# An mLSTM cell with a SwiGLU feed-forward: a new start-up order, M and decay spread from bf16 parts, wider weight pieces, the third group's k and q by 32x32 tiles, the last result by columns

## The chip, the cores and the metric

The kernel runs on one core of a Trainium2 chip (trn2). Time is the device time of one execution in microseconds (us). Before the change it is 604.95 us (median of 3 runs, 604.86 to 605.26).

Engines: PE = TensorE, PEld = its weight loads, DVE = VectorE, ACT = ScalarE, POOL = GpSimd, SP = SyncE, which here only issues transfers. L12 is line 12 of that kernel; the same statement has another line number in another kernel.

## The reference

```python
# q, k, v, o_gate: (4, 8, 768, 40) float32; i_gate, f_gate: (4, 8, 768) float32
for t in range(S):                                   # the mLSTM cell
    m_new  = np.maximum(f_gate[:, :, t] + m, i_gate[:, :, t])
    f_stab = np.exp(f_gate[:, :, t] + m - m_new)
    i_stab = np.exp(i_gate[:, :, t] - m_new)
    C = f_stab * C + i_stab * np.einsum('bhd,bhe->bhde', vt, kt)
    n = f_stab * n + i_stab * kt
    h_tilde = np.einsum('bhde,bhe->bhd', C, qt)
    denom = np.maximum(np.abs((n * qt).sum()), 1.0)
    y[:, :, t] = sigmoid(o_gate[:, :, t]) * h_tilde / denom
x = y.transpose(0, 2, 1, 3).reshape(3072, 320)       # the bridge
g = x @ w_gate                                       # (320, 1536)
out = (g * sigmoid(g) * (x @ w_val)) @ w_out         # (1536, 320)
# [cut: axes of broadcasting.] The three weights arrive as float64.
```

## The kernel before

The cell is computed in chunks of 128 steps. A unit is one batch entry and one chunk, 24 in all, and three units make a group. The program is a start-up, in which the first two groups of the cell, the conversion of all weights from float64 and the first group of the feed-forward are done, and then seven more groups.

Each piece of work is a Python generator, and a string says which generator makes its next step. Each engine executes its instructions in that order, so the string is the schedule. Names in it: `R` loads a weight piece, `C` converts it, `kq` loads k and q, `T` turns (transposes) them, `M` and `E` spread M (the running maximum, `m` in the reference) and the decay, that is, copy one head's row to all partitions, `S` scores, `F` finish of a unit, `H` gate and value products, `J` the products with w_out.

```python
START = """
pad0 kq1*2 pad0 bar1 v1 pad1 bar2 kq1 pad2 pad4 kq1 pad4 pad5 pad2 which kq0*2 runA v2 ... [cut]
"""

def convert(n):                       # float64 bits to float32: ACT twice, DVE three times, POOL once
    ...
    nc.scalar.activation(bits, hi.bitcast(F32), AF.Abs)
    nc.scalar.activation(low, lo, AF.Identity, scale=2.0 ** -51, bias=two_c)
    yield
    nc.vector.tensor_scalar(bits, bits, scalar1=2.0 ** -15, scalar2=None, op0=ALU.max)
    nc.vector.tensor_scalar(bits, bits, scalar1=3, scalar2=None, op0=ALU.logical_shift_left)
    nc.vector.scalar_tensor_tensor(size, in0=hi, scalar=0x80000000, in1=bits, ...)
    yield
    nc.gpsimd.tensor_tensor(place(*key).bitcast(U32), low, size, op=ALU.add)   # wgv_sb or wo_sb
    yield

def spread_m(u):                      # one head's row of M to all 128 partitions, float32
    ...
            nc.tensor.matmul(units[u]["mb"][two][:, j, :], lhsT=idb[:, h:h + 1].to_broadcast([BH, 128]),
                             rhs=M_sb[:, c, :], start=False, stop=True, skip_group_check=True)

def turn(u, tag):                     # k and q: four PE transposes each, one ACT copy each
    ...
            for j in range(PR):
                nc.tensor.transpose(tp[:, j, :], un[name][:, 2 * j:2 * j + 2, :]..., ident)
            yield
            nc.scalar.copy(un[name + "T"], tp)
            yield

def project(g, i, part):              # h times w_out, a third of the contraction at a time
    ...
    for m in range(part * n, (part + 1) * n):
        nc.tensor.matmul(p, lhsT=h_ring[...], rhs=wo["sb"][:, m, :], start=(m == 0), stop=(m == NFC - 1))
    yield
    if part == 2:
        nc.scalar.copy(z, p)
        yield
        nc.sync.dma_start(out=out[ds(g * TW + i * 128, 128), :].rearrange("(t four) d -> four t d", four=NSQ), in_=z)
        yield
```

The groups from the fourth on already take k and q another way: loads that lay 32x32 tiles side by side, which DVE then transposes (`load_x`, `turn_x`). A float32 matmul instruction shows as two PE records in these traces.

## Time and profile before

| | before |
|---|---|
| median of the first 3 runs | 604.95 us |
| span of the profiled run | 603.9 us |
| PE busy | 580.7 us (96%) |
| first feed-forward products of units 1 and 2 (t0) | 62.4 us |
| first products of the second group (g2) | 139.1 us |
| second group | 66.9 us, PE without a gap |
| DVE, ACT, POOL busy | 52%, 38%, 28% |

At **t0** the matmuls of the form 64x256 begin, the feed-forward of units 1 and 2. At **g2** the second group begins; from there to the end PE works back to back. Shares of busy time over the whole span say little here: DVE at 52% looks idle, yet it decides t0.

### The profile page before, as it was taken

Reading aid. Unit: us, or ns where it says so; the run is one execution under the profiler, and the core shown is the slowest. Engines: PE = TensorE matmul, PEld = TensorE weight load, DVE = VectorE, ACT = ScalarE, POOL = GpSimd, SP = SyncE. Lnnn points to the kernel's source line nnn. Section 1 sums busy time; section 2 is a strip of 40 time slices with the busy share of each in tenths; the row PEclk is TensorE's granted clock in tenths of the full one; section 3 lists DMA queues with packets and bytes.
Section 4 is the critical chain, followed back from the end, with each engine's and each line's share of the span. In section 5 each row is a group of like instructions: output and inputs, shape, how many; then the busy total and the mean of one; then the engine's idle time right before and its main releaser. Section 6 shows DMA issues by size and latency. Waiting matters only on the chain.

```text
span 603.9 us, 11003 instructions
## 1 busy us (share of the span) xinstructions
PE 580.7 (96%) x4132; PEld 393.9 (65%) x4132; DVE 316.0 (52%) x742; ACT 227.8 (38%) x484; POOL 167.2 (28%) x236
## 2 busy tenths in 40 slices
PE   7877899999999999999999999999999999999996
PEld 5665666766657666776667666766677666766564
DVE  7289778972457345552467245644466334633310
ACT  3736799974215321433224411542143411111100
POOL 4235565570213221251213222151114211220000
PEclk9878799999999999999999999999999999999999
DMA  9798999504631166104651267005740300010000
GB/s 134 199 127 187 213 206 219 150 13 93 109 89 41 55 113 120 64 12 90 91 111 47 64 109 138 36 11 106 106 116 13 90 18 0 3 30 4 1 6 26
DMA packets 150612, 50.74 MB, mean 84 GB/s; under 512 B 126592, under 2 KB 145376, under 8 KB 150432
## 3 DMA queue, kind: packets, MB, share of 16 engines
q1 hardware_dynamic: 150560, 50.05, 40.8%
q8 instruction: 32, 0.52, 0.4%
q14 instruction: 20, 0.16, 0.1%
HBM read 45.91 MB, written 4.11 MB: 83 GB/s over the span
## 4 chain that ended last, share of the span: by engine, by line
PE 85%; DVE 5%; DMA 3%; ACT 2%; POOL 2%; issue 1%; SPq 1%; DVEq 0%; ACTq 0%; POOLq 0%
PE gv_ps L605 48%; PE o_ps L624 23%; PE yT L517 5%; PE sp L498 3%; PE add L543 2%; PE mb L443 2%; PE tp_kq L486 1%; DMA raw<-in_moe_w_out_dram 1%; POOL wo_sb L297 1%; DMA e_bc<-e_dram 1%; DMA v<-in_v_dram 1%; ACT w_sb L472 1%; DMA out_dram<-z_sb 1%; DVE size L293 0%; DVE bits L292 0%
## 5 line engine op out<-in xcount | busy, mean ns | idle before, releaser
L605 PE MATMUL gv_ps<-xT,wgv_sb 64*128 64x384 f32 (+2 forms) x1980 | 323.5, 480 | 9.7 <-DVE xT L591 3.5
L605 PEld LDWEIGHTS gv_ps<-xT,wgv_sb 64*128 64x128 f32 x1980 | 193.2, 192 | 126.2 <-POOL wgv_sb L297 6.4
L624 PE MATMUL o_ps<-wo_sb,h_ring 128*128 128x320 f32 x576 | 158.0, 434 | 0.9 <-POOL wo_sb L297 0.7
L612 DVE TENSOR_TENSOR sg<-sg,gv_ps 128x384 f32<-128x384 f32 x84 | 46.5, 554 | 182.9 <-ACT sg L609 182.9
L624 PEld LDWEIGHTS o_ps<-wo_sb,h_ring 128*128 128x128 f32 x576 | 108.5, 190 | 48.1 <-POOL wo_sb L297 1.8
L609 ACT ACTIVATE sg<-gv_ps 128x384 f32<-128x384 f32 (+2 forms) x99 | 47.6, 481 | 233.5 <-PE gv_ps L605 233.4
L577 POOL TENSOR_TENSOR yb<-yb,o 128x512 f32<-128x512 f32 x24 | 30.4, 1267 | 120.5 <-DVE yl L576 120.5
L613 DVE TENSOR_TENSOR h_ring<-sg,gv_ps 128x384 f32<-128x384 f32 (+2 forms) x99 | 53.5, 541 | 12.7 <-ACT sg L609 3.2
L506 POOL TENSOR_TENSOR qT<-qT,e_bc 128x512 f32<-128x512 f32 x18 | 22.9, 1274 | 118.1 <-PE sp L498 58.2
L472 ACT ACTIVATE w_sb<-w_sb,g_T 128x128 f32<-128x128 f32 x168 | 51.1, 388 | 6.3 <-POOL w_sb L468 6.2
L584 ACT COPY yb<-yb 32x512 f32<-32x512 f32 x24 | 14.8, 616 | 60.3 <-POOL yb L577 60.0
L502 DVE TENSOR_TENSOR w_sb<-sp,w_sb 128x512 f32<-128x512 f32 x48 | 31.0, 684 | 7.5 <-POOL v_w L477 4.5
L468 POOL TENSOR_SCALAR_AFFINE_SELECT w_sb<-w_sb 128x1024 f32<-128x1024 f32 x21 | 22.9, 1091 | 41.6 <-DMA w_sb<-M_dram 40.9
L591 DVE STREAM_TRANSPOSE xT<-yb 128x512 f32<-128x512 f32 x24 | 17.1, 710 | 31.0 <-POOL yb L584 30.2
L498 PEld LDWEIGHTS sp<-qT,kT 64*128 64x128 f32 x384 | 27.1, 199 | 6.1 <-issue 0.7
L498 PE MATMUL sp<-qT,kT 64*128 64x128 f32 x384 | 28.7, 287 | 0.1
L629 ACT COPY z_sb<-o_ps 128x320 f32<-128x320 f32 x24 | 10.1, 421 | 48.2 <-issue 25.3
L202 POOL COPY lo<-o 32x128 f32<-32x128 f32 x48 | 19.0, 395 | 33.4 <-ACT o L199 29.5
L517 PE MATMUL yT<-w_sb,v 128*64 128x128 f32 x384 | 27.5, 282 | 0.0
L297 POOL TENSOR_TENSOR wgv_sb<-low,size 128x512 uint32<-128x512 uint32 (+1 forms) x16 | 19.2, 1201 | 21.6 <-DVE size L293 20.6
L517 PEld LDWEIGHTS yT<-w_sb,v 128*64 128x64 f32 x384 | 23.8, 141 | 1.1 <-issue 1.1
L564 DVE STREAM_TRANSPOSE yb<-yT 128x256 f32<-128x256 f32 x48 | 18.8, 427 | 7.4 <-PE yT L517 7.4
(87 smaller groups left out, 436.2 us busy)
## 6 DMA issues: line engine op xcount, KB each, us to landing
w_sb<-M_dram SPq DMA_DIRECT2D x21, 512.0 KB
e_bc<-e_dram SPq DMA_DIRECT2D x36, 128.0 KB
k<-in_k_dram SPq DMA_DIRECT2D x48, 80.0 KB
v<-in_v_dram SPq DMA_DIRECT2D x24, 160.0 KB
o<-in_o_gate_dram SPq DMA_DIRECT2D x48, 80.0 KB
raw<-in_moe_w_out_dram SPq DMA_DIRECT2D x8, 480.0 KB
out_dram<-z_sb SPq DMA_DIRECT2D x24, 160.0 KB
raw<-in_moe_w_gate_dram SPq DMA_DIRECT2D x24, 128.0 KB
```

The costliest lines, as they stand in the source:

```text
L297: nc.gpsimd.tensor_tensor(place(*key).bitcast(U32), low, size, op=ALU.add)
L468: nc.gpsimd.affine_select(w, w, compare_op=ALU.is_ge, fill=-NEG, base=0, pattern=[[0, H], [1, L]], channel_multiplier=-1)
L472: nc.scalar.activation(w[:, h], m[h], AF.Exp, bias=g_T[:, c, b * H + h:b * H + h + 1], scale=-1.0)
L498: nc.tensor.matmul(sps[two][:, j, :], lhsT=un["kT"][r, j, :], rhs=un["qT"][r, j, :], start=True, stop=True)
L502: nc.vector.tensor_tensor(w2, un["sp"][two], w2, op=ALU.mult)
L517: nc.tensor.matmul(un["ys"][two][col * HP:(col + 1) * HP, (h % PR) // 2, :], lhsT=lhsT, rhs=rhs, start=(two, col) in un["fresh"], stop=las ...
L577: (nc.gpsimd if u in GATED else nc.vector).tensor_tensor(yb, yb, un["o"].rearrange("p x (four d) -> p x four d", d=D)[:, :, :, 0:32], op=A ...
L605: nc.tensor.matmul(ps[i][:, cols], lhsT=wgv_sb[r, kc, ts(m, 128)], rhs=xts[g][r, kc, cols], start=(kc == 0), stop=(kc == NKC - 1))
L609: nc.scalar.activation(sg[:, cols], ps[0][:, cols], AF.Sigmoid if g else AF.Silu)
L612: nc.vector.tensor_tensor(sg[:, cols], sg[:, cols], ps[0][:, cols], op=ALU.mult)
L613: nc.vector.tensor_tensor(h_ring[:, (g * NFC + m) % NH, cols], sg[:, cols], ps[1][:, cols], op=ALU.mult)
L624: nc.tensor.matmul(p, lhsT=h_ring[:, (g * NFC + m) % NH, ts(i, 128)], rhs=wo["sb"][:, m, :], start=(m == 0), stop=(m == NFC - 1))
```

## The change

The start-up loses PE passes (float32 spreading, 24 transposes), gets wider weight loads, and an order in which four conversions come early and ACT changes its table less often. The last result is written in two column halves.

Core of the diff (cuts marked `...`):

```diff
-    f_sb = gates.tile([BH, NB, L], F32)
-    nc.sync.dma_start(out=f_sb, in_=f_gate.rearrange("b h (c t) -> (b h) c t", t=L))
+    f_sb = gates.tile([128, NB, L], F32)          # copies in partition quarters 0, 2, 3
+    for c0, c1, quarters in ((0, GC, (0, 2, 3)), (GC, NB, (0,))):
+        for r in quarters:
+            for t, a in ((f_sb, f_gate), (i_sb, i_gate)):
+                (nc.scalar if r else nc.sync).dma_start(out=t[r * BH:(r + 1) * BH, c0:c1], in_=...)
...
+    def upper(t):                                 # the upper 16 bits of each float32, as bf16
+        return t.bitcast(BF16).rearrange("p c (t two) -> p c t two", two=2)[:, :, :, 1]
+
+    def parts(t, n):                              # quarter 2: the rest, quarter 3: the rest of that
+        for r in (64, 96):
+            x = t[r:128, 0:n]
+            nc.vector.tensor_tensor(x, x, upper(x), op=ALU.subtract)
+        yield
...
     def spread_m(u):                              # spread_e likewise
-                nc.tensor.matmul(units[u]["mb"][two][:, j, :], lhsT=idb[:, h:h + 1].to_broadcast([BH, 128]),
-                                 rhs=M_sb[:, c, :], start=False, stop=True, skip_group_check=True)
+                nc.tensor.matmul(units[u]["mb"][two][:, j, :], lhsT=ones(h, 128),
+                                 rhs=upper(M_sb)[:, c, :], start=False, stop=True, skip_group_check=True)
...
+        if m < 2:
+            piece("gv", 0, PR, m * 128, 128)
+        elif m % 2 == 0:
+            for a in range(0, PR, 2):
+                piece("gv", a, 2, m * 128, 256)   # was: PR blocks of rows, 128 columns
...
-            nc.scalar.copy(un[name + "T"], tp)
+            if u in first and name == "k":
+                nc.vector.tensor_copy(un["kT"], tp)
+            else:
+                nc.scalar.copy(un[name + "T"], tp)
...
+            if c > 0 and u in early:              # the C update of the first two groups
+                nc.gpsimd.tensor_tensor(kept, old[:, :, 0:D1], d, op=ALU.mult)
+                yield
+                nc.vector.tensor_tensor(new[:, :, 0:D1], add, kept, op=ALU.add)
...
-            nc.vector.tensor_copy(den[p:p + 32], den[p + 32:p + HP])
+            (nc.gpsimd if u in early else nc.vector).tensor_copy(den[p:p + 32], den[p + 32:p + HP])
...
+    def project_last(g, i):
+        n = DM // 2
+        for c, copy in enumerate((nc.scalar.copy, nc.vector.tensor_copy)):
+            for m in range(NFC):
+                nc.tensor.matmul(p, lhsT=h_ring[...], rhs=wo["sb"][:, m, ts(c, n)], ...)
+            yield
+            copy(z, p)
+            yield
+            dst = out[ds(g * TW + i * 128, 128), ts(c, n)].rearrange("(t four) d -> four t d", four=NSQ)
+            for r in range(NSQ):
+                (nc.sync if r % 2 else nc.scalar).dma_start(out=dst[r], in_=z[r * 32:(r + 1) * 32])
+            yield
...
-    for u in first + second + third:              # T: PE transposes
+    for u in first + second:
         stream(f"kq{u}", load_kq, u)
         stream(f"T{u}", turn, u, "cell")
+    stream("X", place_x)
+    for n in range(4):
+        stream(f"x{n}", load_x, 2, n)
+    for u in third:
+        stream(f"k{u}", load_k, u)
...
+        if g == 1:
+            for n, u in enumerate(third):
+                stream(f"t{n}", turn_x, u)
+        play(GROUP1 if g == 1 else GROUP, streams)
```

The string START is new as a whole, and GROUP1 is GROUP with the third group's turning and k loads placed in the second group.

## The prediction

> **What bounds the kernel now.** I read the page's busy table and the 40 slices first, then a table of stretches, the chain, the matmul groups by shape, and last the order of PE and DVE instructions in time over the first 140 us.
>
> ```profile
> PE   7877899999999999999999999999999999999996
> ACT  3736799974215321433224411542143411111100
> PEclk9878799999999999999999999999999999999999
> DMA  9798999504631166104651267005740300010000
> ```
>
> PE is full from the fifth slice to the last but one. Only the first four slices (60 us) have gaps, and there the clock dips too.
>
> The stretches (columns: window, length, then busy us of PE, PEld, DVE, ACT, POOL with counts, granted clock, DMA share, GB/s):
>
> ```profile
> 0.00:20.00 20.00, 16.03 (x70) 12.30 (x71) 12.73 (x40) 6.89 (x18) 7.77 (x34) 1.00 0.99 156
> 20.00:62.40 42.40, 30.57 (x317) 25.22 (x316) 30.07 (x73) 25.88 (x52) 18.29 (x24) 0.78 0.90 167
> 62.40:100.00 37.60, 37.50 (x270) 25.17 (x272) 29.93 (x57) 33.38 (x60) 21.67 (x24) 0.93 0.99 206
> 123.60:139.20 15.60, 15.05 (x66) 10.46 (x66) 8.80 (x17) 10.49 (x23) 9.38 (x12) 1.00 0.12 30
> 139.20:206.10 66.90, 66.90 (x490) 44.78 (x490) 33.98 (x84) 21.72 (x50) 16.08 (x22) 1.00 0.35 72
> ```
>
> The kernel has a start-up (0 to 139.2 us: the first two groups of the cell, conversion of all weights, the first group of the feed-forward, transposes for the third group) and seven further groups. The last line is one such group: PE 66.90 of 66.90 us. Six full groups, a shorter last one and the tail make 603.9 - 139.2 = 464.7 us, all PE back to back. DVE, ACT and POOL have room in it and nothing they win there is time. So the question is when the start-up ends.
>
> Inside the start-up the PE timeline shows the gaps (start, length, what, in brackets the idle before it and its releaser):
>
> ```profile
> 7.40 3.78 PE L443 MATMUL mb<-f_sb,ident 32*128 32x128 f32 x16 [0.74 <-DVE f_sb L358]
> 13.01 3.78 PE L443 MATMUL mb<-f_sb,ident 32*128 32x128 f32 x16
> ...
> 43.21 1.94 PE L605 MATMUL gv_ps<-xT,wgv_sb 64*128 64x128 f32 x20 [2.96 <-DVE C L549]
> ...
> 53.66 4.36 PE L605 MATMUL gv_ps<-xT,wgv_sb 64*128 64x128 f32 x40 [2.78 <-POOL wgv_sb L297]
> ...
> 62.38 7.22 PE L605 MATMUL gv_ps<-xT,wgv_sb 64*128 64x256 f32 x40 [3.47 <-DVE xT L591]
> ```
>
> At 62.4 the feed-forward of units 1 and 2 begins; it waits for DVE's xT, the end of `finish` of unit 2. After that PE hardly idles. I call this moment t0. DVE was busy 12.73 + 30.07 = 42.8 us before it, so idle for nearly 20, mostly between 10 and 30 us while PE spread M in float32 and ACT waited for that.
>
> **What the Trainium skill says.** (1) "FP8 and Floating Point Precision", TensorE Precision Notes: true FP32 takes 4 passes of the array. The trace agrees: an o_ps instruction of 320 columns is two records, 72 records in 19.59 us, so 0.54 us an instruction, or 4 x 320 columns at 2.35 per ns. (2) "TensorE: Matmul & The Clock Gate", What's actually happening: the array runs at 1.2 GHz until about 3.4 us of sustained work, then at 2.4. It agrees: 16 mb records take 3.78 us early, 0.236 us each, twice the 0.107 us of two passes of 128 columns at full clock. (3) "DMA: Bandwidth & Descriptors", Why small descriptors are slow: a fixed cost per packet. The trace: 6636 packets, nearly all 160 bytes, went at 128 GB/s in the first 10 us at a full share; around 20 to 30 us, with 1 KB rows, 189 GB/s at 0.80. (4) "ScalarE: Activation LUTs", Table sets: each change of set costs a load, about 2.7 us there; here each is 1.28 us. The measurement decides.
>
> **The change part by part.**
>
> M and decay: the spreading matmul becomes bf16 over 128 partitions (three exact parts, one pass). Before:
>
> ```profile
> L443 PE MATMUL mb<-f_sb,ident 32*128 32x128 f32 x48 | 10.0, 381 | 0.7 <-DVE f_sb L358 0.7
> L454 PE MATMUL e_ps<-e_sb,ident 32*64 32x128 f32 x32 | 3.1, 348 | 0.1
> L486 PE MATMUL tp_kq<-ident,k 128*128 128x128 f32 x36 | 7.1, 332 | 1.4 <-DVE f_sb L351 1.2 <-DVE w_sb L502 0.2
> ```
>
> After: 24 mb records of perhaps 0.11 to 0.16 us cold (estimate: one pass), 3 us instead of 10, and 16 of e, 1.5 instead of 3.1. It costs four DVE subtractions of about 0.5 us, two ahead of the first M spread, which moves from 7.4 to about 9.1 us; but all 24 can then be done by about 14 us where the last now ends at 22.6.
>
> Third group in 32x32 tiles: 24 PE transposes go, 24 x 0.148 us (4 in 0.59) = 3.6 us of PE at the end or middle of the saturated part, so worth their time in full. Six ACT copies of 0.59 us go too, and 1.5 us around 137 to 139 us where transposes waited for those copies. In their place 12 DVE transposes of 0.43 us in the second group, where DVE has 33 us free, and small-packet loads that have some 30 us until they are needed.
>
> Weight pieces of 256 columns: same bytes in 2 KB rows. 5.2 of the 7.9 MB of gate and value weights; 230 GB/s to perhaps 300 (estimate from the packet times above), 5 us of DMA time. Natural k, q of the third group leave the busy stretch too, 6 x 164 KB at 128 GB/s, 7.7 us.
>
> Order of the start-up: rewritten. Four conversions now come before the first score product on DVE, filling the hole of 10 to 30 us. ACT changes table 14 times instead of 18 before the second group, 5.1 us less; its work up to the last conversion falls from 101.5 to 81.4 us (counts by group times mean durations). DVE's falls from 102.7 to 96.7: den copies and half of the C update go to POOL, kT copies and the parts come.
>
> Now t0. In the new DVE order the work up to xT of unit 2 is 51.7 us by the same means; for before the same count gives 46.4 where the trace has 42.8 (neighbours overlap), so 47.7 us. Starting at 1 us with no idle that is 48.7. Following the order by hand through M, W, scores, copies and `finish`, with the durations of before, I find waits of only 1.5 to 2 us (a POOL-and-ACT tail in `finish`), 50.5. Everything slips a little, and PE will be cold: I take t0 = 53.5 against 62.4.
>
> PE work left after t0, at warm times (64x384: 0.161 us a record; x256: 0.108; o_ps 0.272; sp 0.89, yT 0.67, add 0.8 per 16):
> before: 180 x 0.161 + 60 x 0.108 + 72 x 0.272 + 36 transposes x 0.148 + sp 1.8 + yT 4.0 + add 1.6 = 67.8; 62.4 + 67.8 = 130.2, the real end was 139.2, so 9 us lost (cold clock after the gap near 3, conversions and table loads).
> after: the same without 32 of the transposes, with 1.5 us of unit 0's third piece: 64.6. With less load on ACT I take 6 us lost. 53.5 + 64.6 + 6 = 124.1. The last conversion would be at about 53.5 + 45 x 0.93 + 3 = 98, well ahead of the last products that need it.
>
> So the start-up gives 139.2 - 124.1 = 15.1 us: 8.9 from t0, 3.2 from work removed, 3 from fewer stalls.
>
> Last result by columns: two passes of 12 instructions with 160 columns. Their matmul would be 0.133 us a record, but the same weights must be loaded twice, and a 128x128 f32 transpose, load and pass, takes 0.148. So 48 x 0.148 = 7.1 against 24 x 0.272 = 6.5 us, +0.6 or up to +2.5 if the load's 0.19 us record is its rate. The tail after the last matmul (598.5 to 603.9) gains a shorter copy and half the bytes in the last transfer, perhaps 0.6. Net +0.5.
>
> Sum: 604.95 - 15.1 + 0.5 = 590.4; I say **590**.
>
> **The rivals.** (a) The early gain is taken up by a new wait: conversions placed early on in-order DVE stall everything if the weights, now sharing the first 20 us of a saturated DMA with k, q, v, come late (DMA share is already 0.99 in 0 to 20). Four pieces are 2 MB, about 9 us of DMA, and unit 1's k, q queue behind them. Then t0 stays at 59 to 62, only the removed work and the stalls count: 597 to 599. (b) PE isn't the limit after t0 but DVE is: 42 us of work in the 42 us of PE work before the o_ps; if PE waits for conversions as in before, the loss stays 9 us: 593 to 594. (c) All goes as in the hand-walk, t0 50.5 and loss 4: 585. (d) DMA binds: its share in before sums to about 110 us up to the last weight piece; minus 5, minus 7.7, minus v and w loads moved behind, it is near 90, so hidden.
>
> **Range and chances.** t0 is uncertain by 4 us, the loss by 3, the tail by 1: **583 to 598** should hold it 8 times in 10. 2% is 592.9. Faster by over 2%: 0.68; within: 0.31; slower: 0.01, since groups two to eight keep their PE work to the instruction.
>
> **What would show it.** mb x24 bf16, under 4 us and the last done before 16; the first x256 feed-forward matmuls at 50 to 57; DVE idle before them under 8 us; the second group's first matmul at 120 to 129, each later group 66.9 us; o_ps x160 records near 0.148. I am wrong if PE waits in the first 60 us for a DMA of raw weights or k, q, if the second group idles for the 32x32 loads, or if the last column parts take 2 us more than before.

## The result, and the profile after

The changed kernel took **586.38 us** (median of 4 runs, 584.98 to 586.90), beside 605.11 us for the kernel before on the same chip (4 runs). The ratio is 0.968 (95%: 0.965 to 0.971). A ratio is the mean time of one kernel's fast runs over that of the other's fast runs of the same rounds, so not quite the ratio of the medians. The prediction of 590 was 3.6 us too high, inside its range.

The page's slices after the change, 14.6 us each (busy tenths of PE and of ACT, and of the DMA engines):

```profile
PE   4797999999999999999999999999999999999997
ACT  2768789832125313341153222542153321111110
DMA  8998997455470566126710465115720300010001
```

PE is at nine tenths from the fifth slice to the last but one, as before, but a slice is shorter. ACT's dense stretch ends with the eighth slice instead of the ninth. The DMA engines are full until the sixth.

The table of stretches of the changed kernel (columns as in the prediction):

```profile
0.00:20.00 20.00, 10.16 (x60) 6.77 (x60) 17.78 (x49) 8.61 (x21) 8.14 (x32) 1.00 0.94 178
20.00:54.10 34.10, 28.21 (x274) 23.21 (x274) 28.33 (x62) 25.03 (x50) 21.46 (x38) 1.00 0.94 183
...
121.20:188.20 67.00, 67.00 (x489) 46.25 (x488) 35.05 (x88) 19.31 (x43) 15.86 (x22) 1.00 0.46 82
```

In the first 20 us DVE is busy 17.78 us where it was 12.73: the hole while PE spread M in float32 is filled. Up to t0 DVE works 17.78 + 28.33 = 46.1 of 54.1 us. The last line is the second group, as full as before.

The PE timeline of the changed kernel (start, length, what, idle before it and its releaser):

```profile
9.95 1.01 PE L504 MATMUL mb<-f_sb,ones_of 128*128 128x128 bf16 x8 [2.03 <-DMA q<-in_q_dram]
...
16.78 0.61 PE L504 MATMUL mb<-f_sb,ones_of 128*128 128x128 bf16 x4
...
54.08 5.88 PE L676 MATMUL gv_ps<-xT,wgv_sb 64*128 64x256 f32 x48 [0.94 <-DVE xT L662]
60.45 15.67 PE L676 MATMUL gv_ps<-xT,wgv_sb 64*128 64x384 f32 x92 [0.50 <-POOL wgv_sb L332]
...
121.24 8.98 PE L676 MATMUL gv_ps<-xT,wgv_sb 64*128 64x384 f32 x54
```

The last spread of M ends at 17.4 us; before it was 22.6. t0 is 54.08 us and g2 121.24.

The groups by shape of the changed kernel (busy us, mean ns of one):

```profile
L504 PE MATMUL mb<-f_sb,ones_of 128*128 128x128 bf16 x24 | 3.3, 307 | 2.0 <-DMA q<-in_q_dram 2.0
L515 PE MATMUL e_ps<-e_sb,ones_of 128*64 128x128 bf16 x16 | 1.1, 264 | 0.4 <-DVE w_sb L566 0.4
L711 PE MATMUL o_ps<-wo_sb,h_ring 128*128 128x160 f32 x48 | 6.7, 299 | 0.0
```

Spreading M and the decay costs PE 4.4 us instead of 13.1.

The spans differ by 603.9 - 584.3 = 19.6 us, and the two moments split that exactly: 62.38 - 54.08 = **8.3 us before t0**; (139.13 - 62.38) - (121.24 - 54.08) = **9.6 us between t0 and g2**; the remaining **1.7 us after g2**.

To see the middle part, here is that same stretch, t0 to g2, of each kernel. Of before:

```profile
62.38:139.13 76.75, 74.83 (x508) 51.46 (x509) 60.87 (x118) 66.86 (x124) 44.10 (x47) 0.96 0.70 156
```

And of the changed kernel:

```profile
54.08:121.24 67.16, 66.66 (x497) 47.16 (x497) 53.56 (x101) 55.93 (x110) 47.49 (x58) 1.00 0.78 184
```

The traces show PE at two speeds: four transposes of one form take 1.12 us at one place of the changed kernel (35.48) and 0.66 at another (43.48). Records at the faster speed are called warm here, at the slower one cold. The prediction counts 67.8 us of warm PE work there before and 64.6 after (an estimate from warm record lengths). Before, PE idles 76.75 - 74.83 = 1.9 us and its records are together 74.83 - 67.8 = 7.0 us longer than warm ones: 9.0 lost. After, it idles 0.5 us and the records are 2.1 us longer: 2.6 lost. ACT's busy time in the stretch fell from 66.86 to 55.93 us.

A part of the 7.0 is not the order's. In the traced run of the kernel before, PE was cold just after t0: the granted clock there was 0.52, which makes 5.62 x 0.48 = 2.7 us:

```profile
62.38:68.00 5.62, 5.62 (x28) 4.57 (x30) 4.32 (x8) 2.96 (x7) 4.20 (x5) 0.52 1.20 180
```

The first 40 records of the form 64x256 took 7.22 us there (in the prediction); in d_m below, with the same 3.5 us of idle before them and the same order after them, they took 4.59. What decides whether this cold stretch comes was not found; it did not come in the changed kernel.

Now the end. The DMA view of the last 6 us of the kernel before (598 to 604 us, 40 slices of 0.15 us; share in tenths of 16 engines, and GB/s):

```profile
DMA  0000000000000012221223222222200000000000
GB/s 0 0 0 0 0 0 0 0 0 0 0 0 0 0 34 43 17 26 17 77 94 94 77 102 102 94 102 102 102 9 0 0 0 0 0 0 0 0 0 0
```

The same view of the changed kernel, 580.5 to 584.4 us (slices of 0.1 us):

```profile
DMA  0000000000000000266103751000000000000000
GB/s 0 0 0 0 0 0 0 0 0 0 0 0 0 0 0 0 53 164 158 46 0 85 184 125 26 0 0 0 0 0 0 0 0 0 0 0 0 0 0 0
```

Before, the final transfer is 160 KB in one piece; it runs for some 2.4 us, most of it at about 100 GB/s, on two tenths of the engines. After, two short bursts of up to 184 GB/s and seven tenths. From the end of the last copy to the end of the span it took 4.9 us before and 3.0 after.

### The profile page after: what moved, and what is told of

Same layout as the page of the kernel before. It is cut to its first block, busy times and chain, and to the rows that moved or that the text cites. A ratio compares the mean times of both kernels' runs of the same rounds, so it can differ in the third digit from the quotient of the medians.

```text
span 584.3 us, 10996 instructions
## 1 busy us (share of the span) xinstructions
PE 564.6 (97%) x4092; PEld 386.0 (66%) x4092; DVE 316.1 (54%) x736; ACT 217.4 (37%) x471; POOL 174.1 (30%) x258
## 4 chain that ended last, share of the span: by engine, by line
PE 89%; DMA 6%; SPq 4%; issue 0%; POOL 0%; DVE 0%; DVEq 0%; POOLq 0%
PE gv_ps L676 52%; PE o_ps L695 26%; PE yT L581 5%; PE sp L562 3%; DMA raw<-in_moe_w_gate_dram 2%; DMA v<-in_v_dram 2%; PE add L607 2%; SPq L170 2%; SPq L301 1%; PE o_ps L711 1%; DMA M_dram<-f_sb 1%; SPq L288 1%; DMA f_sb<-in_f_gate_dram 0%; SPq L219 0%; SPq L211 0%
## 5 line engine op out<-in xcount | busy, mean ns | idle before, releaser
L676 PE MATMUL gv_ps<-xT,wgv_sb 64*128 64x384 f32 (+2 forms) x1980 | 316.7, 474 | 1.4 <-DVE xT L662 0.9
L676 PEld LDWEIGHTS gv_ps<-xT,wgv_sb 64*128 64x128 f32 x1980 | 190.6, 187 | 115.9 <-issue 2.8
L695 PE MATMUL o_ps<-wo_sb,h_ring 128*128 128x320 f32 x552 | 151.5, 435 | 0.0
L695 PEld LDWEIGHTS o_ps<-wo_sb,h_ring 128*128 128x128 f32 x552 | 104.2, 190 | 43.8 <-issue 1.7
L684 DVE TENSOR_TENSOR h_ring<-sg,gv_ps 128x384 f32<-128x384 f32 (+2 forms) x99 | 53.6, 541 | 9.9 <-ACT sg L680 1.2
L533 ACT ACTIVATE w_sb<-w_sb,g_T 128x128 f32<-128x128 f32 x168 | 50.8, 387 | 14.8 <-POOL w_sb L529 14.7
L529 POOL TENSOR_SCALAR_AFFINE_SELECT w_sb<-w_sb 128x1024 f32<-128x1024 f32 x21 | 22.9, 1092 | 56.6 <-DMA w_sb<-M_dram 55.8
L655 ACT COPY yb<-yb 32x512 f32<-32x512 f32 x24 | 14.8, 616 | 52.5 <-POOL yb L648 52.2
```

Of the source, the lines that this page charges most:

```text
L529: nc.gpsimd.affine_select(w, w, compare_op=ALU.is_ge, fill=-NEG, base=0, pattern=[[0, H], [1, L]], channel_multiplier=-1)
L533: nc.scalar.activation(w[:, h], m[h], AF.Exp, bias=g_T[:, c, b * H + h:b * H + h + 1], scale=-1.0)
L676: nc.tensor.matmul(ps[i][:, cols], lhsT=wgv_sb[r, kc, ts(m, 128)], rhs=xts[g][r, kc, cols], start=(kc == 0), stop=(kc == NKC - 1))
L684: nc.vector.tensor_tensor(h_ring[:, (g * NFC + m) % NH, cols], sg[:, cols], ps[1][:, cols], op=ALU.mult)
L695: nc.tensor.matmul(p, lhsT=h_ring[:, (g * NFC + m) % NH, ts(i, 128)], rhs=wo["sb"][:, m, :], start=(m == 0), stop=(m == NFC - 1))
```

## The experiments

All kernels of one call ran on the same chip beside the kernel before, whose median was 605.44, 605.53 and 605.70 us in the three calls. An interval of a ratio is about 0.3% either way, some 2 us, so four kernels within 2 us of the changed one cannot be told apart by their totals; for these I use the moments of the trace. Traces of one order also differ: the changed kernel and u_last, with the same start-up, have t0 at 54.1 and 52.4. d_third and d_third2 have the order of the kernel before up to t0 but for one load of k, and yet t0 is 65.2 and 64.8, not 62.4. They leave it at about 20 us, where the same eight records are cold in them and not in the kernel before (PE timelines of the kernel before and of d_third2):

```profile
19.69 1.28 PE L443 MATMUL mb<-f_sb,ident 32*128 32x128 f32 x8
...
19.71 2.07 PE L450 MATMUL mb<-f_sb,ident 32*128 32x128 f32 x8
```

So a t0 from one trace is uncertain by some 2 us. A label beginning with u takes the changed kernel and undoes one part, d takes the kernel before and adds parts; loads6 and best2 are edits of the changed kernel.

| kernel | median us | ratio (95%) | t0 | t0 to g2 | g2 to g3 | g3 to end |
|---|---|---|---|---|---|---|
| before | 605.1 | 1 | 62.4 | 76.8 | 66.9 | 397.8 |
| changed | 586.4 | 0.968 (0.965 to 0.971) | 54.1 | 67.2 | 67.2 | 395.9 |
| u_last | 587.3 | 0.969 (0.966 to 0.972) | 52.4 | 69.0 | 67.2 | 397.4 |
| u_cols | 586.3 | 0.967 (0.965 to 0.970) | 53.6 | 66.7 | 67.2 | 395.9 |
| u_m32 | 587.9 | 0.969 (0.967 to 0.972) | 54.8 | 67.0 | 67.2 | 396.2 |
| u_third | 592.3 | 0.978 (0.975 to 0.981) | 54.0 | 73.6 | 68.1 | 396.0 |
| u_moves | 588.7 | 0.972 (0.971 to 0.974) | 55.8 | 67.4 | 67.2 | 395.9 |
| loads6 | 592.1 | 0.979 (0.976 to 0.981) | 53.6 | 74.7 | 67.2 | 396.2 |
| best2 | 588.2 | 0.971 (0.970 to 0.973) | 53.1 | 69.1 | 67.2 | 397.8 |
| d_m | 600.1 | 0.993 (0.990 to 0.996) | 58.1 | 74.2 | 66.9 | 397.7 |
| d_third | 621.3 | 1.026 (1.023 to 1.029) | 65.2 | 73.8 | 84.8 | 398.0 |
| d_third2 | 604.8 | 1.001 (0.998 to 1.004) | 64.8 | 72.7 | 67.2 | 398.4 |
| d_parts | 615.4 | 1.018 (1.015 to 1.021) | 58.6 | 72.7 | 84.5 | 396.8 |
| d_parts2 | 598.0 | 0.989 (0.986 to 0.992) | 58.6 | 72.7 | 67.2 | 397.1 |

(t0, g2 and g3, the first products of the third group, are read from the PE timeline of each profiled run.)

### u_last: the last result whole again

```diff
-            if g == NG - 1 and n >= 3 * (GC - 1):
+            if False:
```

> The changed kernel with the last result in one piece again (12 products of 320 columns, one copy, one transfer). My prediction gave the columns +0.6 us on PE and -0.6 us in the tail. The two traces say +0.15 us on PE (48 records in 6.68 us) and 3.4 instead of 5.4 us after the last matmul, so this should be slower by 1.5 to 2.0 us: about 588.2. Rival (the tail is only the fixed latency of a transfer, and the 2 us are chance): within 0.5 us of 586.4. The start-up must end at 121 us as before.

Measured: 587.26 us. The total cannot tell it from 586.38, but the stage can: from g3 to the end 397.4 against 395.9, so the column parts are worth 1.5 us. It is not the matmuls: the 48 records of 160 columns took 6.68 us on the timeline (0.139 each), and a third of a normal unit-by-unit block of 72 records, 19.59 us in the kernel before, is 6.53. Loading the same weights twice as often cost nothing that shows. The Trainium skill, "TensorE: Matmul & The Clock Gate", Step-by-step: what each phase is for, says that PE pulls the next weight load ahead while a matmul runs; the trace agrees, with weight-load records of 190 ns beside matmuls that follow each other every 139 ns.

So it is the transfer. The Trainium skill, "DMA: Bandwidth & Descriptors", Why a DMA increments its semaphore by 16 and not by 1, says that the number k of engines is the largest number up to 16 that divides the slowest dimension of both access patterns. The old transfer is written four x 32 x 320, so 4 engines; a new one is 32 x 160, so 16. The trace agrees: two tenths and 102 GB/s before, up to seven tenths and 184 GB/s after. best2 below tests it. A whole result of 320 columns in four such transfers, without the halves, was not run.

### u_cols: weight pieces of 128 columns again

```diff
-                piece("gv", a, 2, m * 128, 256)
+                piece("gv", 0, PR, (m + a // 2) * 128, 128)
```

> The changed kernel with all gate and value pieces of 128 columns and 1 KB rows, same number, same order. Theory: DMA is hidden after t0, and before t0 the four first pieces land in time, so within 1 us of 586.4; DMA share in the first 100 us rises by 4 to 6 us of engine time. Rival (the wide rows carry the gain, because the weights feed the early conversions): t0 later by 3 us or more, 589 to 592.

Measured: 586.31 us, as expected, and the DMA share of the first 100 us rose from 0.96 to 1.00. Wider pieces are worth nothing here. More than that: the small wait at 60.45 us of the changed kernel is gone in this one. There POOL came early to what it needs (POOL timeline):

```profile
55.57 0.75 POOL L538 TENSOR_TENSOR v_w<-v,w_sb 128x328 f32<-128x328 f32 x1 [1.04 <-DMA v<-in_v_dram]
```

In the changed kernel the same instruction starts at 58.43. Its chain of waits between 47 and 61 us shows why that matters (start, length, what):

```profile
47.34 10.96 DMA v<-in_v_dram
...
58.44 0.74 POOL v_w L538
59.18 1.23 POOL wgv_sb L332
...
60.45 1.55 PE gv_ps L676 x7
```

The load of v for unit 3 takes 11 us in the full queue; POOL, in order, waits for it and only then writes the converted weights that PE needs. With u_last, where t0 was 1.7 us earlier, PE waited all of it there (PE timeline):

```profile
60.40 15.87 PE L676 MATMUL gv_ps<-xT,wgv_sb 64*128 64x384 f32 x92 [2.02 <-POOL wgv_sb L332]
```

So 60.4 us is a new barrier: in these traces an earlier t0 bought nothing where v of unit 3 landed no earlier.

### u_m32: the spreading in float32 again, in the new order

```diff
-        for r in (64, 96):
-            x = t[r:128, 0:n]
-            nc.vector.tensor_tensor(x, x, upper(x), op=ALU.subtract)
         yield
...
-                nc.tensor.matmul(..., lhsT=ones(h, 128), rhs=upper(M_sb)[:, c, :], ...)
+                nc.tensor.matmul(..., lhsT=idb[:, h:h + 1].to_broadcast([BH, 128]), rhs=M_sb[0:BH, c, :], ...)
```

> The changed kernel, its order kept, with M and decay spread in float32 as before and without the four subtractions. Theory (the float32 spread was on the path to t0): the three units' spreads take 9 to 10 us of cold PE instead of 3.3, DVE waits for the scores, t0 goes from 54.1 to 57 to 60 us, total 589 to 592. Rival (with early conversions filling DVE the spread is hidden, and DVE's own work sets t0; without the subtractions it even saves 2 us): 584.5 to 587.

Measured: 587.91 us, below the theory's range and above the rival's; t0 54.8, only 0.7 us later, although PE spends the old time on it, 3.78 us for 16 records again (PE timeline):

```profile
8.12 3.78 PE L501 MATMUL mb<-f_sb,ident 32*128 32x128 f32 x16 [0.20 <-DVE f_sb L401]
```

DVE then sits idle for 6.2 us in one go (DVE timeline):

```profile
24.55 0.33 DVE L621 COPY C<-add 128x164 f32<-128x164 f32 x1 [6.19 <-PE add L604]
```

Yet it has less to do: the subtractions are gone, M is ready earlier (spreading starts at 8.12 instead of 9.95), and in the first 54 us it works 42.8 us instead of 46.0. The new order had already taken most of what the float32 spreading cost.

### u_third: the third group's k and q by PE transposes again

```diff
-    for u in first + second:
+    for u in first + second + third:
         stream(f"kq{u}", load_kq, u)
         stream(f"T{u}", turn, u, "cell")
-    stream("X", place_x)
-    ...                                   # load_x, load_k, turn_x of the third group
+ START: its X and x steps out, kq6 kq7 kq8 for k6 k7 k8, and T7*4 T8*4 T6*4 at the end
```

> The changed kernel with the third group's k and q loaded by tokens again and turned by 24 PE transposes at the end of the start-up. Theory: PE does 24 x 0.148 = 3.6 us more where it is full, plus some 1.5 us of waits for the copies: start-up ends 3.6 to 5.1 us later, 590 to 591.5. Rival (there was slack that the transposes fill, or the loads of 32x32 tiles cost the second group as much): under 2 us.

Measured: 592.26 us, 5.9 more, nearly all between t0 and g2 (73.6 against 67.2). The PE timeline just ahead of g2:

```profile
121.43 0.60 PE L534 MATMUL tp_kq<-ident,k 128*128 128x128 f32 x4
...
125.24 0.63 PE L534 MATMUL tp_kq<-ident,q 128*128 128x128 f32 x4 [1.88 <-DMA q<-in_q_dram]
```

Six such groups take 6.2 us there (121.43 to 127.59): 3.6 us of transposes and the rest waits, 1.9 us of them for one load of q. That wait comes from the place that this run gives its loads. So in the new order this part is worth some 4 us, and 6 with that wait.

### d_m: only the bf16 spreading, in the kernel before

```diff
+    [gates in three quarters, upper(), parts(), ones(), as in the change]
- ... tgA decA kq0 M1 decA ...
+ ... tgA decA mp kq0 M1 decA ...
- ... kq2 runB ...
+ ... kq2 runB ep ...
```

> The kernel before, its order kept, with only the bf16 spread of M and decay in three parts (gates in 128 rows included). Theory: the spreads shrink from 10 to about 3.3 us of cold PE, scores and t0 come earlier by 3 to 6 us (62.4 to 57-59), total 599 to 602. Rival (without the new order DVE waits elsewhere, for raw weights or copies, so t0 hardly moves): 604 to 605.

Measured: 600.13 us, 5.4 less by the medians. t0 falls from 62.4 to 58.1 (PE timeline):

```profile
58.08 4.59 PE L637 MATMUL gv_ps<-xT,wgv_sb 64*128 64x256 f32 x40 [3.48 <-DVE xT L623]
```

The bf16 parts are worth about 4 us in the old order (0.990 to 0.996, so 2 to 6) and about 1 in the new one. As I read it, the two remove the same idle time of DVE.

### d_third: only the third group's tiles, in the kernel before

```diff
- START: kq6 kq7 kq8 and T6 T7 T8
+ START: X*4 x0*8 x1*8 x2*8 x3*8 k6*2 k7*2 k8*2 after C22, ahead of the feed-forward's last steps
```

> The kernel before with only the third group's k, q in 32x32 tiles, turned by DVE in the second group. Theory: 3.6 us of transposes and 1.5 us of waits at the end of the start-up go, 600 to 601.5. Rival: the tile loads, issued late in this order, make the second group wait and give it back: 603 to 606.

Measured: 621.25 us, 16 more than before. This was my placement, not the idea. The PE timeline of the second group:

```profile
157.88 18.47 PE L612 MATMUL gv_ps<-xT,wgv_sb 64*128 64x384 f32 x97 [14.78 <-ACT z_sb L636]
```

PE waits 14.8 us for ACT's copy of a result, and ACT for the store of the one before it: the 38 small-row loads stood ahead of the result stores in the one in-order SP queue, and nothing needed them yet.

### d_parts: spreading, tiles and column parts, in the kernel before's order

```diff
+    [the edits of d_m and of d_third, and project_last]
```

> The kernel before with bf16 spread, third group's tiles and last result by columns, but the start-up order, the weight pieces, and the division between engines of before. If the parts carry the gain and add up: 605 - 4 - 5 - 2 = 594. What is missing to 586.4 is what the new order and the moves among engines are worth: I expect 6 to 10 us, that is 592 to 597.

Measured: 615.42 us. The same wait stands in it, 15.4 us, and the second group takes 84.5 us instead of 66.9, so it says nothing on the sum of the parts. Both were repeated with other places for the loads.

### loads6: six more table loads on ACT between t0 and g2, in the changed kernel

```diff
         nc.scalar.activation(sg[:, cols], ps[0][:, cols], AF.Sigmoid if g else AF.Silu)
+        if g == 0 and m in (4, 6, 7):                        # spare: a column of its own
+            nc.scalar.activation(spare, two_c, AF.Exp)
         yield
```

Each of the three one-column exponentials forces a load of its table and one of the table that comes back, 1.28 us each in the trace: 7.7 us of ACT.

> The changed kernel with six more table loads on ACT (a one-column exp between silu at three feed-forward pieces after t0), 6 x 1.28 = 7.7 us of ACT. Theory (the loss after t0 fell from 9 to 2.5 us mostly because ACT is relieved): start-up ends 3 to 6 us later, 589 to 592. Rival (ACT had slack; the loss was clock and conversions): under 1.5 us.

Measured: 592.11 us, 5.7 more; t0 to g2 grew by 7.5 us (74.7 against 67.2). The stretch in its own trace:

```profile
53.56:128.26 74.70, 70.55 (x496) 47.90 (x496) 53.55 (x101) 64.20 (x119) 47.48 (x58) 0.98 0.77 169
```

DVE, POOL and the transfers have the same work as in the changed kernel, ACT 8.3 us more. PE idles 4.2 us, up from 0.5, and its records, 70.55 us against 66.66, are 3.9 us longer for the same work. Where PE stops, it names ACT (PE timeline):

```profile
90.02 2.53 PE L677 MATMUL gv_ps<-xT,wgv_sb 64*128 64x256 f32 x19 [1.31 <-ACT sg L681]
```

So ACT, loaded at these three places, is almost one to one on the path. Not all of the 3.9 us is PE waiting: between 71 and 75 us, after a wait of 1.2 us for ACT, the granted clock was 0.57, which is 1.7 us. Some 2.2 us remain that are neither idle nor clock. A record of the form 64x384 is shown 0.49 us long and a new one starts every 0.161, so a short gap between starts does not show as idle; that the 2.2 us are such gaps was not traced.

### d_third2: the tiles again, their loads between and behind the stores

```diff
- ... C22 C23 C22 X*4 x0*8 x1*8 x2*8 x3*8 k6*2 k7*2 k8*2 W6 J4 ...
+ ... C22 C23 C22 X*4 x0*8 W6 J4 ... x1*2 J8*2 x1*6 x2*2 F4*2 ... J5*2 x2*6 x3*8 k8*2 k7*2 k6*2
```

> The kernel before with only the third group's k, q in 32x32 tiles, as in the run that came out 16 us slower, but with the tile loads placed between and behind the stores of the first group's results, where that run had all 38 of them ahead of the stores and PE waited 15 us for a buffer that a store held. Theory (the loss was the place of the loads in the one in-order issue queue): 600 to 602, the wait gone. Rival (the small-packet loads themselves are too slow at this point): still above 606.

Measured: 604.83 us (0.998 to 1.004), not the expected 600 to 602. The placement was the whole loss of d_third: 16 us are gone. But nothing is gained in the total, where the same part is worth 4 to 6 us in the new order. The two traces differ in more than the tiles: t0 is 2.4 us later (the cold records above), and the stretch from t0 to g2 is 4.0 us shorter, of which 2.7 is the cold stretch that only the kernel before had. That leaves about 1.3 us for the tiles. With the transposes out of the way PE waits earlier, 2.4 us in all for conversions of w_out, where it was 0.7 (PE timeline):

```profile
131.41 6.19 PE L631 MATMUL o_ps<-wo_sb,h_ring 128*128 128x320 f32 x22 [1.68 <-POOL wo_sb L304]
```

### d_parts2: all three parts in the old order, loads placed as in d_third2

```diff
+    [the edits of d_m and of d_third2, and project_last]
```

> Bf16 spread, tiles for the third group and last result by columns in the kernel before, with its start-up order, pieces and engines, tile loads placed as in the run above. If the parts add up: 605.3 - 5.4 - 4.5 - 0.9 = 594.5; the rest to 586.4, some 8 us, would be the new order with its fewer table loads. If the new order matters little: 587 to 589. If the loads are the trouble: above 600.

Measured: 597.96 us, ratio 0.989, where the adding up had given 594.5. So the parts alone give some 7 us of the 19; the remaining 11.6 to 586.38 need the new order, the moves between engines and the pieces. Its stretch from t0 to g2:

```profile
58.57:131.26 72.69, 68.93 (x485) 47.16 (x485) 58.55 (x114) 63.86 (x118) 45.92 (x51) 1.00 0.63 151
```

PE idles 3.8 us and its records, 68.93 us against an estimate of 67.8 - 24 x 0.148 = 64.25 warm, are 4.7 longer: 8.4 lost, a number like that of the kernel before, but made up otherwise. There is no cold stretch here (granted clock 1.00), and of the 3.8 us of idle PE waits 2.4 for POOL's conversions of w_out, 1.0 for ACT and 0.3 for DVE. ACT works 63.9 of the 72.7 us, 7.9 more than in the changed kernel. With the parts but without the order, the loss is large, and ACT is not the only engine that PE names in it.

### u_moves: the work moved between engines moved back

```diff
-            if u in first and name == "k":
+            if False:
...
-            if c > 0 and u in early:
+            if False:
...
-            (nc.gpsimd if u in early else nc.vector).tensor_copy(den[p:p + 32], ...)
+            nc.vector.tensor_copy(den[p:p + 32], ...)
```

> The changed kernel with the work moved between engines put back: the first group's kT copies on ACT, the C update in four scalar_tensor_tensor on DVE, the den copies on DVE. DVE has about 2 us more up to t0, ACT 1.8. Theory (DVE and ACT are the bound up to t0 and shortly after): 588 to 590. Rival (they had slack there): 586 to 587.

Measured: 588.71 us, 2.3 more, and t0 55.8, 1.7 later. The moves are worth about 2 us, and the trace puts them before t0 (traces of one order differ there by as much).

### best2: a try at something better

```diff
+    nc.scalar.activation(spare, two_c, AF.Exp)               # the table of exp loaded at the very start
...
-            nc.vector.memset(q_ring[r][:, :, D:], 0.0)       # pads of q and k from DVE to ACT
+            nc.scalar.activation(ring[r][:, :, D:], ..., AF.Copy, scale=0.0)
...
-            for r in range(NSQ):
-                (nc.sync if r % 2 else nc.scalar).dma_start(out=dst[r], in_=z[r * 32:(r + 1) * 32])
+            for r in (0, 2):                                 # two transfers for a column part, not four
+                (nc.sync if r else nc.scalar).dma_start(out=dst[r:r + 2], in_=z[r * 32:(r + 2) * 32])
```

> The changed kernel with three additions aimed at what the traces show is left: the exp table loaded at the start by a one-column exp (1.28 us of load stood on the way to the first weights at 10.3 us), the zero pads of k and q written by ACT, idle until 10 us, rather than by DVE (1.9 us of DVE ahead of the first scan), and the last column part stored by two transfers rather than four (0.4 us of issue). If DVE's work up to t0 is the bound, t0 comes 1.5 to 2.5 us earlier and the tail is 0.4 shorter: 583.5 to 585. Rival (raw weights or the cold PE set the pace up to t0): 585.5 to 587.

Measured: 588.20 us, not the expected 583.5 to 585, and no better than the changed kernel. ACT's first exponential of the score weights came 1.8 us earlier (9.79 us), and t0 was 53.1, but POOL met the barrier of u_cols again (POOL timeline):

```profile
58.14 0.75 POOL L539 TENSOR_TENSOR v_w<-v,w_sb 128x328 f32<-128x328 f32 x1 [4.20 <-DMA v<-in_v_dram]
```

g2 came at 122.1, so the earlier start was worth nothing there. The end got longer by 1.9 us (g3 to end 397.8 against 395.9). The DMA view of its last 5.7 us:

```profile
DMA  1111100000000111111110111111100000000000
GB/s 49 45 45 45 45 14 0 0 0 0 0 0 4 18 13 45 45 27 36 27 27 18 40 45 45 45 49 45 40 5 0 0 0 0 0 0 0 0 0 0
```

Each transfer is now written 2 x 32 x 160. The same halves, the same copies, half the number of transfers, and the rate is 45 GB/s on one tenth of the engines: two engines, as the rule says. With the halves kept, the end is as long as that of the kernel before (397.8 us from g3 in both): the column parts gain by the slowest dimension of their transfers, 32, and not by the halves alone.

## Why the prediction was right, and where its terms were not

**What bounds the kernel: right.** The gain lies before g2 and in the last microseconds. The second group is 67.2 us after and 66.9 before.

**t0 = 53.5: right** (54.08), to the half microsecond by luck. The mechanism held: the DVE idle up to t0 fell from nearly 20 to 8.0 us, at the edge of the predicted "under 8". But DVE worked 46.1 us where the sum had 47.7, and idled 8.0 where it had 53.5 - 47.7 = 5.8, so two errors cancel, and t0 moves by some 2 us between traces anyway. The last spread of M ended at 17.4 us, later than the predicted 14 to 16, because the first began at 9.95 and not at 9.1 and because the rest now follow the order of other work; u_m32, with its spreads later still, moved t0 by 0.7 us only. At 9.95 the trace names a load of q, and a PE wait for k or q was the prediction's own sign of being wrong. DVE's subtractions, which the spread needs, end at 8.76 + 1.15 = 9.91, so it is them, and the sign did not come true there (DVE timeline):

```profile
8.76 1.15 DVE L436 TENSOR_TENSOR f_sb<-f_sb 64x384 f32<-64x384 f32 x2
```

The prediction's check of the clock was too kind: its 0.107 us is an estimate from the pages' figures, 0.236 is 2.2 times that, and in the trace the same records warm up only to 0.144 (8 in 1.15 at 21.49). mb cost 3.3 us (predicted 3), e 1.1 (1.5). What the runs add is that the credit is shared: the bf16 parts alone give 4.3 us of t0 in the old order (d_m), but taking them out of the new order costs 0.7 (u_m32), and the moves are worth 1.7 (u_moves), each from single traces. A cause that removes idle time is worth what idle time is left.

**Work removed, 3.2 us: right as far as it can be read.** u_third needs 3.6 us for its 24 transposes, and the rest of its 5.9 us are waits, 1.9 of them for a load that this run placed late.

**"With less load on ACT I take 6 us lost": the direction right, the size wrong.** The loss after t0 is 2.6 us, not 6; it was 9.0. This term is off by 3.4 us. I had put near 3 us of the 9 down to a cold clock, and that was right: it is 2.7. That part is gone in the changed kernel, and not because of ACT: d_m, with the old order and ACT's work at 66.7 us, did not have it either and lost 74.2 - 67.8 = 6.4. The other 3.7 us of the fall (9.0 - 2.7 - 2.6) are what less load on ACT, or earlier conversions, can have healed. ACT can hold this stretch up: adding 7.7 us of table loads lengthened it by 7.5 (loads6). The parts in the old order, with ACT's 63.9 us of work and no cold stretch, lost 8.4 (d_parts2), but most of the idle time that PE shows there is waiting for POOL, the last step of conversions that begin on ACT. The whole change took 10.9 us off ACT in this stretch, 7.9 of them beyond what the parts alone did. That an added load hurts is shown; that the removal of ACT work is what healed these 3.7 us is not. How much is ACT's load, how much the earlier places of the conversions and how much fewer table loads was not separated.

**"Net +0.5" for the last result: wrong, in sign too.** It is -2.0 us: the tail from the last matmul to the end went from 5.4 to 3.4 us, and the matmuls cost nothing. Both halves of the term failed. I took the weight load for a limit at 160 columns (0.148 us a record, 0.139 measured), and for the tail I counted bytes and a shorter copy (0.6 us), where the tail gained 2.0 us by the number of DMA engines (best2). With 0.3 us lost in the second group, what lies after g2 is -1.7, 2.2 us better than the term.

The terms together: 590.4 + 0.6 (t0) - 3.4 (loss) - 2.2 (end) = 585.4, near the measured 586.38. Both errors were on the same side.

**The rivals.** (a) Conversions that wait for early weights did not hold t0. But a load did become the next bound, one the rival did not name: v of unit 3 at 60.4 us. (b) DVE as the limit after t0, loss 9: no; DVE works 53.6 of 67.2 us and the loss is 2.6. (c) 585 with t0 50.5 and a loss of 4: the total is closest, by luck; the terms are not. (d) DMA hidden: right for the weights, u_cols gives the same time; not quite for the one load of v.

**What stays open.** By subtraction the new order alone is worth 11.6 - 2.3 (moves) - 0 (pieces) = about 9 us, but it was never run without the moves and the pieces, and parts and order overlap. By this subtraction the order is the largest share of the gain, and its cause is argued from the traces, not isolated. No run was left for the version that the findings point to: the load of v for unit 3 earlier in the queue, the early exp table and pads of best2, and the four transfers of the last halves kept. Nothing shown here beats the changed kernel by more than the noise. The 2 us by which PE records after t0 are still longer than warm ones were not traced further.

## What to carry to other kernels

Ask of each part what idle time is left when the other parts are in: the third group's tiles were worth 4 to 6 us in one order and about 1 in another, the bf16 parts 4 and 1. Where PE looks full, add a known load to an engine beside it and see whether the stretch grows by as much; that found ACT on the path at three places where PE showed little idle. Look for cold records before comparing two traces: they moved single stretches here by 2 to 3 us. Write a small final transfer so that its outermost dimension is a multiple of 16, and put loads that nobody needs yet behind the stores in an in-order queue.

## What the Trainium skill lacked or had wrong

- "ScalarE: Activation LUTs", Table sets: about 2.7 us for a change of table. Here a load took 1.28 us: 1283 ns is the mean of the 15 in the first 140 us of the changed kernel and of the 21 in loads6. The page's section What ACT_TABLE_LOAD costs has the same 1283 ns for the load and adds a drain of about 1380 ns; that drain does not show here. In loads6 the activation before a load ends at 80.14 us, the load runs from 80.16 to 81.44, and the next activation starts at 81.45.
- "TensorE: Matmul & The Clock Gate", What's actually happening: two speeds, the faster one after about 3.4 us of sustained work. The two speeds are in the traces, the time is not: PE is busy for 12.30 of the 12.30 us from 7.40 to 19.70 in the kernel before until its records get shorter, and in d_third2 for 19.38 of 19.38 us from 7.42 to 26.80, with records still long (8 in 2.07 us at 22.76).
- The same page, Seeing it yourself, warns that the clock events of a trace have been seen to be unreliable, and here is a case: in the stretch from 20 to 54.1 us of the changed kernel the granted clock reads 1.00, and four transposes of one form take 1.12 us at 35.48 and 0.66 at 43.48. Just after t0 in the kernel before the clock (0.52) and the records agree.
- "TensorE: Matmul & The Clock Gate", Step-by-step: a reader of a trace would need to be told that a weight load's record, 190 ns, is no rate: matmuls with a new weight each followed every 139 ns.
- No page that I found gives a size for what a busy PE can hide: in loads6 the same work had records 3.9 us longer in sum, of which the granted clock explains 1.7.
